# Seven products over two steps, two alternating banks, sums without GpSimd, weights kept as differences

## Chip, cores and metric

The kernel runs on one core of a Trainium2 chip. The metric is device time in microseconds: 755.94 us in the median of three runs (754.37 to 757.52). One further execution was recorded by the hardware profiler; it took 754.39 us.

## Reference

Two parts follow each other. The first is an attention with 32 memory slots per head (batch 8, 8 heads, 576 rows, head width 64):

```
a = softmax(phi)                 # over the 576 rows, per slot
k_m = a^T k ; v_m = a^T v        # 32 slots per head
attn = softmax(q k_m^T / 8)      # over the 32 slots
x = attn v_m                     # laid out as (4608, 512)
```

The second is a gated network on all 4608 rows, with weights of 512 x 1536 (two) and 1536 x 512:

```
out = (sigmoid(x w_gate) * (x w_val)) w_out
```

All arrays are fp32. The kernel never builds x: it multiplies v_m into the weights of gate and value first (that product is called U) and then multiplies U by the turned attention matrix `at`.

## The kernel before, in words

Every fp32 operand of the large matmuls is split into two fp32r parts, hi and lo (`x = hi + lo`), and every product is three matmuls: hi with hi, hi with lo, lo with hi. A hi part is a cast on ScalarE (ACT), a lo part a subtraction on VectorE (DVE).

The hidden width of 1536 is worked in 12 blocks f of 128, the rows in batch elements b of 576. The first stage does b = 0 to 3, in turns of four blocks for one element; the order of its instructions on DVE and ACT is planned at build time, except where the code chains them. Partial output sums go to DRAM and come back through four buffers called `row` (`row_of`, `leave`), stored from GpSimd's (POOL) queue and loaded on the queue of SyncE (SP). On the steps that begin with the third turn of b = 0 the weights of two blocks each are copied to DRAM (`kept_w`, six stores of 1 MB, L1188), also on SP, which works in order.

The second stage does b = 4 to 7, twelve steps each, one (b, f) after the other; the loop begins at L1301. `step` chains each engine's instructions in the order in which the code lists them, so PE, DVE, ACT and POOL each work in order there. For these elements gate and value of a block are computed together, as a 2 x 2 block product with seven products in place of eight (Winograd's form): the 576 rows in two halves of 288, gate and value as the two halves of the other side. `raw_at` holds the four blocks of the turned attention matrix and four sums of them (`sums_at`); `pair_u` makes U of two neighbouring blocks with 16 small matmuls into two PSUM banks, `u_out` copies them out (r and l), `u_sums` forms their sums (s), `part_hi` and `part_lo` split r, l and s. A pair is made one step ahead of its use.

The class `Group` is one step. `first` computes four products into banks c, d, a, b:

```
self.product(self.c, "s1", "t1", True)     # P5
self.product(self.d, "s3", "t3", True)     # P7
self.product(self.a, "a11", "b11", True)   # P1
self.product(self.bb, "s2", "t2", True)    # P6
```

`copies` moves P5, P7 and P1 to SBUF on ACT; `base` adds P6 and P1 on DVE; `corner` adds P5, P7 and that base on POOL (two adds); `second` adds P3, P4 and P2 onto banks c, d and a; `add` adds the base to c and d on DVE. `gate` takes the two sigmoids on ACT, `product_of` multiplies value by gate on DVE, `to_hi`, `to_left` and `to_lo` split the result. `out_half` multiplies a finished block by the output weights: two output tiles of 128 rows, three matmuls of 512 columns each, into four banks `acc`. In even steps two tiles stand between `first` and `second`, in odd steps none (L1330). `late_sides` spreads the softmax, the turning and the memory of the next two elements over the steps of the present one; `LEFT_AT` places the output of the 64 left-over rows of each element (`out_left`, 12 matmuls of 512 columns at a time).

POOL does the two adds of `corner`, the four sums of `u_sums`, the lo part of r and `sums_at` (L1145, L1146, L1076 to L1079, L1086, L931 to L934).

Of the kernel before, what the change touches and what calls it, by code (L numbers as in the profile page):

```python
# [17 lines left out]
P = 128  # L18
# [3 lines left out]
NKT = 4  # L22
# [76 lines left out]
def attn_moe_kernel(  # L99
# [27 lines left out]
    def bank():  # L127
        if "banks" in pools:
            return late_bank("b")
# [319 lines left out]
    def scores(b, c):  # L449

        n = cut(b, c).stop - cut(b, c).start
        pb = [late_bank("a"), late_bank("b")] if "banks" in pools else [bank(), bank()]
# [272 lines left out]
    def leave(b, f, t):  # L725
# [3 lines left out]
        if (b, t) in part:  # L729
            nc.vector.tensor_tensor(st, o, st, op=ALU.add)  # L730
            part.pop((b, t))
        elif t % 2:
            nc.scalar.copy(st, o)
        else:
            nc.vector.tensor_copy(st, o)  # L735
# [28 lines left out]
    def out_left(pair, f0, nf):  # L764
# [14 lines left out]
        for x in range(0, DM, n):  # L779
            xs = slice(x, x + n)  # L780
            st, o = left_sum[pair][:, xs], (late_bank("a") if x else bank())[:, :n]
# [256 lines left out]
    def pair_u(n, pb):  # L1038
# [7 lines left out]
        u = pairs_of[n] = {"pb": pb}  # L1046
# [16 lines left out]
    def u_out(n):  # L1063

        u = pairs_of[n]
        u["r"], u["l"] = late_tile("r_raw", 512), late_tile("l_raw", 512)
        nc.scalar.copy(u["r"], u["pb"][1])
        nc.vector.tensor_copy(u["l"], u["pb"][0])

    def u_sums(n, eng):  # L1070

        u = pairs_of[n]
        u["s"] = late_tile("s_raw", 768)
        l, r = [u[x].rearrange("p (f w x) -> p f w x", f=2, w=2) for x in "lr"]
        s = u["s"].rearrange("p (j f x) -> p j f x", j=3, f=2)
        eng.tensor_tensor(l[:, :, 1], l[:, :, 1], r[:, :, 1], op=ALU.add)  # L1076
        eng.tensor_tensor(s[:, 0], l[:, :, 1], l[:, :, 0], op=ALU.subtract)
        for w in range(2):
            eng.tensor_tensor(s[:, 1 + w], r[:, :, w], s[:, 0], op=ALU.subtract)  # L1079
# [4 lines left out]
    def part_lo(n, name, eng=None):  # L1084
        hi, lo = of_pair(n, name)
        (eng or nc.vector).tensor_tensor(lo, pairs_of[n][name], hi.bitcast(F32), op=ALU.subtract)  # L1086

    def operand(n, name, fi):
# [3 lines left out]
            "a11": ("l", fi * 256), "s1": ("l", fi * 256 + P),  # L1092
            "s2": ("s", fi * P), "s4": ("s", 256 + fi * P), "s3": ("s", 512 + fi * P),
# [11 lines left out]
    class Group:  # L1105
# [13 lines left out]
        def first(self):  # L1119
            self.c, self.d, self.a, self.bb = [late_bank(x)[:, :HALF] for x in "cdab"]  # L1120
            self.product(self.c, "s1", "t1", True)
            self.product(self.d, "s3", "t3", True)
            self.product(self.a, "a11", "b11", True)
            self.product(self.bb, "s2", "t2", True)

        def copies(self):
# [3 lines left out]
            self.p7 = late_tile("c_p7", HALF)  # L1130
            self.z = lp[0].tile([P, 4, HALF], F32, name="z", bufs=2)
            nc.scalar.copy(self.p5, self.c)  # L1132
            nc.scalar.copy(self.p7, self.d)  # L1133
            nc.scalar.copy(self.s1, self.a)  # L1134

        def base(self):
            nc.vector.tensor_tensor(self.x, self.bb, self.s1, op=ALU.add)  # L1137

        def second(self):
            self.product(self.c, "s4", "b22", False)  # L1140
            self.product(self.d, "a22", "t4", False)
            self.product(self.a, "a12", "b21", False)

        def corner(self):
            nc.gpsimd.tensor_tensor(self.p5, self.p5, self.p7, op=ALU.add)  # L1145
            nc.gpsimd.tensor_tensor(self.z[:, 3], self.p5, self.x, op=ALU.add)  # L1146

        def add(self, i):
            nc.vector.tensor_tensor(self.z[:, 1 + i], (self.c, self.d)[i], self.x, op=ALU.add)  # L1149

        def gate(self, i):
            curve(self.z[:, i], self.z[:, 1] if i else self.a, AF.Sigmoid)

        def product_of(self):
            nc.vector.tensor_tensor(self.z[:, 2:4], self.z[:, 2:4], self.z[:, 0:2], op=ALU.mult)  # L1155
# [20 lines left out]
    for i, (b, f, at_start, at_end) in enumerate(steps[:MAIN]):  # L1176
# [10 lines left out]
        if 0 <= k < NP:  # L1187
            move(kept_w[k], wg[:, 2 * k : 2 * k + 2].rearrange("p f k n -> p (f k n)"))  # L1188
# [23 lines left out]
        while len(pend) >= LAG:  # L1212
# [3 lines left out]
        if i >= MAIN - 2:  # L1216
            k = i - (MAIN - 2)
            pair_u(k, [bank(), bank()])
            u_out(k)
            u_sums(k, nc.vector)  # L1220
            for name in "lrs":
                part_hi(k, name)
                part_lo(k, name)
            if k == 0:
                out_half(*pend.pop(0))
# [10 lines left out]
    def out_next():  # L1236
        if pend:
            step(out_half, *pend.pop(0))

    def turn_at(b, i):  # L1240
        at_hi(b, i)
        at_lo(b, i)

    def late_sides(b):
# [6 lines left out]

        if n < B:
            soft = [s_max(n, c) for c in range(2)]
            norm = normalize(n)
            for c in range(2):
                put(2 * c + 2, "p", scores, n, c)
                put(2 * c + 2, "p", to_blocks, n, c)
                put(2 * c + 3, "z", next, soft[c])
                put(2 * c + 3, "z", next, soft[c])
            put(6, "a", s_exp, n)  # L1260
            put(7, "z", next, norm)
            put(8, "z", next, norm)
            put(9, "z", cross, n)
            put(10, "a", sums_at, n, nc.gpsimd)
        def go(k=1):
            for _ in range(k):
                next(memories[m])

        def end_n(k=1):
            for _ in range(k):  # L1270
                next(memories[n])

        if QUAD + 1 < n < B:
            put(0, "m", end_n)
            put(0, "mc", end_n, 2)
        if m < B:
# [3 lines left out]
            put(3, "z", a_max, m)  # L1280
            put(6, "a", a_exp, m)
            put(6, "z", a_sum, m)
            put(6, "z", begin_m)
            for f, place in ((7, "m"), (8, "m"), (9, "m"), (10, "m")):
                put(f, place, go)
                put(f, "mc", go)
            if m + 1 < B:
                put(10, "z", load_next, m + 1)
# [3 lines left out]
        (4, 6): (1, 0), (4, 11): (1, 4), (5, 6): (1, 8), (5, 11): (2, 0), (6, 6): (2, 4), (6, 11): (2, 8),  # L1292
        (7, 6): (3, 0), (7, 10): (3, 4),
    }

    for i in (1, 0):
        step(turn_at, QUAD, i)
    raw_at.pop(QUAD)
    load_q(QUAD + 1)
    out_next()  # L1300
    for b, f in [(b, f) for b in range(QUAD, B) for f in range(NFT)]:  # L1301
# [8 lines left out]
        odd = f % 2  # L1310
        turning = f == NFT - 1 and b + 1 < B
        g = Group(b, f)
        step(g.first)
        step(g.copies)
        step(g.base)
        step(g.corner)
        ready = 0 < n + 1 < NPAIRS and n > 0
        busy = f in (6, 7) and b + 1 < B
        if ready and not odd and not busy:
            for name in "rl":  # L1320
                step(part_hi, n + 1, name)
            step(part_lo, n + 1, "r", nc.gpsimd)
            step(part_lo, n + 1, "l")
            step(part_hi, n + 1, "s")
        if ready and odd and busy:
            for name in "lrs":
                step(part_hi, n + 1, name)
            step(part_lo, n + 1, "l")
        side("a")
        if not odd:  # L1330
            out_next()
        step(g.second)
        if (b, f) in LEFT_AT:
            step(next, run_left)
        side("m")
        step(g.add, 0)
        step(g.add, 1)
        step(g.gate, 0)
        if turning:
            step(at_hi, b + 1, 1)  # L1340
        side("mc")
        step(g.gate, 1)
        if turning:
            step(at_lo, b + 1, 1)
            step(at_hi, b + 1, 0)
        if (b, f) in LEFT_AT:
            step(next, run_left)
        if ready and not odd and not busy:
            step(part_lo, n + 1, "s")
        step(g.product_of)  # L1350
        if turning:
            step(at_lo, b + 1, 0)
        out_next()
        side("p")
        if ready and odd and busy:
            step(part_lo, n + 1, "s")
            step(part_lo, n + 1, "r", nc.gpsimd)
        step(g.to_hi)
        if odd and n + 2 < NPAIRS:
            step(pair_u, n + 2, [late_bank("a"), late_bank("b")])  # L1360
            step(u_out, n + 2)
            step(u_sums, n + 2, nc.gpsimd)
        step(g.to_left)
        if turning:
            raw_at.pop(b + 1)
            if b + 2 < B:
                load_q(b + 2)
        step(g.to_lo)
        if odd:
            out_next()  # L1370
        side("z")
        if (b, f + 1) in LEFT_AT:
            run_left = out_left(*LEFT_AT[b, f + 1], TURN)
            step(next, run_left)
        pend.extend((b, f, c, f == 0, f == NFT - 1) for c in range(2))
        if odd:
            pairs_of.pop(n)
# [58 lines left out]
```

## Time and profile before

| | us |
|---|---|
| median of three runs | 755.94 |
| lowest, highest | 754.37, 757.52 |
| the profiled execution | 754.39 |
| its span, first to last instruction | 752.5 |
| PE busy (matmuls) | 715.0, 95% of the span |
| DVE busy | 544.2, 72% |
| ACT busy | 409.4, 54% |
| POOL busy | 246.6, 33% |

Busy time is time in which an engine had an instruction under way. A matmul's end is modelled, and matmuls overlap, so 95% of PE is not 95% of its peak. The second stage begins at 379 us and ends at about 740 us; POOL works in it for 212 us and hardly before it. The granted clock of PE is full but for a few us, 0.98 on average in the stretch from 564.9 to 657.5 us. Every stall is shown by the engine that waits and by what released it.

### The profile page before, as it was taken

Reading aid. Unit: us, or ns where it says so; the run is one execution under the profiler, and the core shown is the slowest. Engines: PE = TensorE matmul, PEld = TensorE weight load, DVE = VectorE, ACT = ScalarE, POOL = GpSimd, SP = SyncE. Lnnn points to the kernel's source line nnn. Section 1 sums busy time; section 2 is a strip of 40 time slices with the busy share of each in tenths; the row PEclk is TensorE's granted clock in tenths of the full one; section 3 lists DMA queues with packets and bytes.
Section 4 is the critical chain, followed back from the end, with each engine's and each line's share of the span. In section 5 each row is a group of like instructions: output and inputs, shape, how many; then the busy total and the mean of one; then the engine's idle time right before and its main releaser. Section 6 shows DMA issues by size and latency. Waiting matters only on the chain.

```text
span 752.5 us, 14249 instructions
## 1 busy us (share of the span) xinstructions
PE 715.0 (95%) x5524; PEld 582.7 (77%) x5524; DVE 544.2 (72%) x907; ACT 409.4 (54%) x937; POOL 246.6 (33%) x289
## 2 busy tenths in 40 slices
PE   8899999999999999999999989999899998898997
PEld 7557788888888898888877767778677787677786
DVE  4999998667787545486478787697776868776554
ACT  4676865455444433354555765647656465464552
POOL 0000100120211011001046466664667556675450
PEclk9999999999999999999999999999999999999999
DMA  8985549567545689232483115612116112141102
GB/s 351 421 352 194 198 143 380 162 225 278 182 161 207 224 311 329 92 105 99 140 329 116 57 57 214 231 58 70 57 57 231 57 57 92 51 153 57 57 1 70
DMA packets 31858, 124.64 MB, mean 166 GB/s; under 512 B 3952, under 2 KB 5232, under 8 KB 25264
## 3 DMA queue, kind: packets, MB, share of 16 engines
q1 hardware_dynamic: 25696, 103.03, 37.6%
q0 software_dynamic: 6096, 20.71, 7.7%
q8 instruction: 43, 0.70, 0.4%
q14 instruction: 23, 0.19, 0.1%
HBM read 94.90 MB, written 28.84 MB: 164 GB/s over the span
## 4 chain that ended last, share of the span: by engine, by line
PE 65%; DVE 16%; ACT 7%; issue 6%; POOL 2%; DMA 2%; SPq 0%; DVEq 0%; ACTq 0%; POOLq 0%
PE acc L189 26%; PE pu_t L189 24%; PE a L189 5%; PE b L189 5%; DVE z L1155 4%; PE c L189 3%; PE d L189 2%; DMA kvm<-in_kvm_dram 2%; DVE z L1149 1%; ACT s_hi L1082 1%; ACT c_p L1132 1%; DVE e L499 1%; DVE e L482 1%; DVE e L473 1%; ACT u_hi L1082 1%
## 5 line engine op out<-in xcount | busy, mean ns | idle before, releaser
L189 PE MATMUL pu_t<-at,u_hi 128*128 128x320 f32 (+1 forms) x752 | 156.1, 303 | 0.2 <-DVE sg L670 0.2
L189 PE MATMUL acc<-wo_hi,g_hi 128*128 128x512 f32 x372 | 151.3, 407 | 0.0
L189 PE MATMUL acc<-wo_hi,g_lo 128*128 128x512 f32 x372 | 146.7, 394 | 0.0
L189 PE MATMUL acc<-wo_lo,g_hi 128*128 128x512 f32 x372 | 146.6, 394 | 0.0
L189 PEld LDWEIGHTS pu_t<-at,u_hi 128*128 128x128 f32 x752 | 124.3, 188 | 11.0 <-issue 2.1
L189 PE MATMUL pu_t<-at,u_lo 128*128 128x320 f32 (+1 forms) x360 | 106.2, 295 | 0.0
L189 PEld LDWEIGHTS acc<-wo_hi,g_hi 128*128 128x128 f32 x372 | 69.9, 188 | 37.6 <-issue 28.5
L164 ACT ACTIVATE sg<-pu_t 128x256 f32<-128x256 f32 (+1 forms) x94 | 38.7, 412 | 81.7 <-PE pu_t L189 81.5
L189 PEld LDWEIGHTS acc<-wo_hi,g_lo 128*128 128x128 f32 x372 | 69.9, 188 | 16.6 <-DVE g_lo L179 0.2
L670 DVE TENSOR_TENSOR sg<-pu_t,sg 128x256 f32<-128x256 f32 (+1 forms) x92 | 41.5, 454 | 52.5 <-ACT sg L164 35.5
L189 PEld LDWEIGHTS acc<-wo_lo,g_hi 128*128 128x128 f32 x372 | 70.1, 188 | 9.1
L1145 POOL TENSOR_TENSOR c_p<-c_p,c_p 128x288 f32<-128x288 f32 x48 | 46.3, 964 | 90.3 <-ACT c_p L1133 90.3
L1160 ACT CAST g_hi<-z 128x512 fp32r<-128x512 f32 x48 | 29.7, 619 | 77.6 <-DVE z L1155 77.6
L175 POOL DMA_DIRECT2D part<-row x32 | 17.7, 555 | 157.9 <-DVE row L735 82.7
L189 PEld LDWEIGHTS pu_t<-at,u_lo 128*128 128x128 f32 x360 | 67.8, 188 | 0.0
L680 ACT CAST g_hi<-sg 128x256 fp32r<-128x256 f32 x90 | 36.5, 407 | 47.9 <-DVE sg L670 46.7
L1155 DVE TENSOR_TENSOR z<-z 128x576 f32<-128x576 f32 x48 | 45.5, 948 | 15.3 <-ACT z L164 12.0
L1146 POOL TENSOR_TENSOR z<-c_p,c_x 128x288 f32<-128x288 f32 x48 | 45.8, 955 | 4.9 <-DVE c_x L1137 1.2
L179 DVE TENSOR_TENSOR g_lo<-sg,g_hi 128x256 fp32r<-128x256 f32 x90 | 37.4, 418 | 12.1 <-ACT g_hi L680 12.1
L1076 POOL TENSOR_TENSOR l_raw<-l_raw,r_raw 128x256 f32<-128x256 f32 x22 | 22.9, 1039 | 66.8 <-ACT left L1170 58.1
L179 DVE TENSOR_TENSOR g_lo<-z,g_hi 128x512 fp32r<-128x512 f32 x48 | 34.1, 710 | 11.2 <-ACT g_hi L1160 11.0
L1137 DVE TENSOR_TENSOR c_x<-b,c_s 128x288 f32<-128x288 f32 x48 | 21.6, 450 | 25.8 <-ACT c_s L1134 25.7
(255 smaller groups left out, 1615.8 us busy)
## 6 DMA issues: line engine op xcount, KB each, us to landing
ring<-wgv SPq DMA_DIRECT2D x24, 1024.0 KB, 4.8
at<-at SPq DMA_DIRECT2D x24, 576.0 KB, 6.3
kvm<-in_kvm_dram SPq DMA_DIRECT2D x12, 1024.0 KB, 10.6
q<-in_qT_dram SPq DMA_DIRECT2D x16, 512.0 KB, 8.2
part<-row POOLq DMA_DIRECT2D x32, 256.0 KB, 4.9
row<-part SPq DMA_DIRECT2D x32, 256.0 KB, 3.9
wgv<-wg SPq DMA_DIRECT2D x6, 1024.0 KB, 10.9
wg<-in_kvm_dram SPq DMA_DIRECT2D x4, 1024.0 KB, 11.7
```

The source lines that it names most:

```text
L164: last_act[0] = nc.scalar.activation(*args, **kw)
L175: last_move[queue] = queues[queue].dma_start(dst, src)
L179: return nc.vector.tensor_tensor(lo, x, hi.bitcast(F32), op=ALU.subtract)
L189: last_pe[0] = do(*args, **kw)
L670: last_prod[0] = nc.vector.tensor_tensor(prod, ps[1][:, :n], sg[:, :n], op=ALU.mult)
L680: nc.scalar.copy(hi, prod[:, : 2 * P])
L1076: eng.tensor_tensor(l[:, :, 1], l[:, :, 1], r[:, :, 1], op=ALU.add)
L1137: nc.vector.tensor_tensor(self.x, self.bb, self.s1, op=ALU.add)
L1145: nc.gpsimd.tensor_tensor(self.p5, self.p5, self.p7, op=ALU.add)
L1146: nc.gpsimd.tensor_tensor(self.z[:, 3], self.p5, self.x, op=ALU.add)
L1155: nc.vector.tensor_tensor(self.z[:, 2:4], self.z[:, 2:4], self.z[:, 0:2], op=ALU.mult)
L1160: nc.scalar.copy(self.g[0], self.z[:, 2:4, : 2 * P])
```

## The change

The seven products of a step get other banks and another order. P1 opens bank d (in odd blocks bank b); ACT copies it (`c_s1`); P6 is added onto the same bank, ACT copies the sum (`c_x`); one step later P7 is added, DVE adds P5 to it (the corner), then P4 is added and DVE multiplies straight out of the bank. P5 opens bank c and P3 is added to it; P2 has bank a alone. So P7 and P4 of a block are computed in the step of the next block, except at an element's last block (f = 11), where they follow at once. `corner`, `base` and POOL's part of `u_sums` and `part_lo` are gone; `copies` is one copy at a time. Both sigmoids read SBUF; the product of value and gate is two operations of 288 columns in place of one of 576.

`pair_u` moves into even steps, one pair ahead, on banks c and a; `u_out` copies both on ACT; `u_sums` is three sums on DVE, since the stored weights already hold a difference: in the `kept_w` copy partitions 0 to 63 hold gate minus value in the columns of value, made by two DVE subtractions into `row` buffers. Each of the six stores becomes four: partitions 64 to 127 whole, the left columns of partitions 0 to 63, and one for each of the two differences.

Output is issued by single tiles (`out_tile`), three or four per step, with sides and left-over work at new places. All finished tiles leave by ACT in the second stage. The second element's pair of the first stage's end (pair 1) is made inside the loop, and queries are loaded at the end of f = 0.

```diff
+        elif t % 2 or "banks" in pools:
             nc.scalar.copy(st, o)
-    def u_sums(n, eng):
...
+    def u_out(n, name):
+        u = pairs_of[n]
+        u[name] = late_tile(f"{name}_raw", 512)
+        nc.scalar.copy(u[name], u["pb"]["lr".index(name)])
+    def u_sums(n, *which):
...
+        for j in which:
+            x, y, op = [
+                (r[:, :, 1], l[:, :, 1], ALU.subtract),
+                (s[:, 0], l[:, :, 0], ALU.add),
+                (r[:, :, 0], s[:, 0], ALU.subtract),
+            ][j]
+            nc.vector.tensor_tensor(s[:, j], x, y, op=op)
...
+        def p(self, n):
+            where, x, t, start = {
+                1: ("d", "a11", "b11", True), 2: ("a", "a12", "b21", True), 5: ("c", "s1", "t1", True),
+                6: ("d", "s2", "t2", False), 3: ("c", "s4", "b22", False), 7: ("d", "s3", "t3", False),
+                4: ("d", "a22", "t4", False),
+            }[n]
+            if start:
+                name = "b" if where == "d" and self.f % 2 else where
+                setattr(self, where, late_bank(name)[:, :HALF])
+            self.product(getattr(self, where), x, t, start)
+        def copy(self, name):
+            nc.scalar.copy(getattr(self, name), self.c if name == "p5" else self.d)
         def add(self, i):
-            nc.vector.tensor_tensor(self.z[:, 1 + i], (self.c, self.d)[i], self.x, op=ALU.add)
+            x, y = {0: (self.a, self.s1), 1: (self.c, self.x), 3: (self.d, self.p5)}[i]
+            nc.vector.tensor_tensor(self.z[:, i], x, y, op=ALU.add)
...
+        def product_of(self, i):
+            x = (self.d, self.z[:, 3])[i]
+            nc.vector.tensor_tensor(self.z[:, 2 + i], x, self.z[:, i], op=ALU.mult)
...
-            move(kept_w[k], wg[:, 2 * k : 2 * k + 2].rearrange("p f k n -> p (f k n)"))
+            w, kept_k = wg[:, 2 * k : 2 * k + 2], kept_w[k].rearrange("p (f k n) -> p f k n", f=2, k=NKT)
+            move(kept_k[D:], w[D:])
+            move(kept_k[:D, :, :, :P], w[:D, :, :, :P])
+            for j in range(2):
+                t = mb.tile([P, DM], F32, name="row", bufs=4)[:D]
+                t = t.rearrange("p (k n) -> p k n", k=NKT)
+                nc.vector.tensor_tensor(t, w[:D, j, :, :P], w[:D, j, :, P:], op=ALU.subtract)
+                move(kept_k[:D, j, :, P:], t)
```

The new step, in its order (h is the group of the block before, `more` means that another pair follows):

```diff
+        if h:
+            step(h.p, 7)
+        step(g.p, 1)
+        if h:
+            step(h.add, 3)
+        step(g.copy, "s1")
...
+        if not odd and more:
+            step(pair_u, n + 1, [late_bank("c"), late_bank("a")])
+            step(u_out, n + 1, "r")
+            step(u_out, n + 1, "l")
+        side("m")
+        side("m3")
+        step(out_tile)
+        if wide:
+            step(out_tile)
+        if h:
+            step(h.product_of, 1)
+        side("act")
...
+        step(g.p, 2)
+        step(g.p, 5)
+        if odd and more:
+            step(part_lo, n + 1, "r")
+        step(g.add, 0)
+        step(g.copy, "p5")
+        if odd and more:
+            step(part_lo, n + 1, "l")
...
+        side("B")
+        if not wide:
+            step(out_tile)
+        if h:
+            step(h.p, 4)
+        step(g.p, 6)
+        if h:
+            step(h.product_of, 0)
+        step(g.copy, "x")
+        if h:
+            step(h.to_hi)
+            step(h.to_left)
+        if not odd and more:
+            step(u_sums, n + 1, 0, 1)
+        step(out_tile)
...
+        step(g.p, 3)
...
+        step(g.add, 1)
...
+        if turning:
+            step(g.p, 7)
+            step(g.add, 3)
+        if h:
+            step(h.to_lo)
+        if turning and b + 1 < B:
+            step(at_lo, b + 1, 0)
+        step(g.gate, 0)
+        step(g.gate, 1)
...
+        if f > 1:
+            step(out_tile)
+        side("Z")
...
+        if turning:
+            step(out_tile)
+            step(g.product_of, 1)
+            step(g.p, 4)
+            if b + 1 < B:
+                step(at_hi, b + 1, 1)
+                step(at_lo, b + 1, 1)
+                raw_at.pop(b + 1)
+            step(g.product_of, 0)
+            step(g.to_hi)
...
```

In `late_sides` the softmax pieces of the next element stand at "B" and "Z" (f = 3 to 9), the scores at "m" of f = 3 and 5, the exponentials at "act" of f = 7, the memory at f = 8 to 11, the crossing at "B" of f = 10.

## Rows read from the trace of the kernel before

**Rows 1.** Stretches b = 4 to 7: length, busy (instructions) by engine, clock, DMA.
```profile
379.20:472.00 92.80, 86.94 (x671) 69.67 (x670) 73.65 (x109) 55.30 (x125) 53.95 (x58) 1.00 0.42 157
472.00:564.90 92.90, 87.12 (x675) 70.17 (x674) 71.16 (x102) 57.53 (x129) 56.74 (x59) 1.00 0.27 96
564.90:657.50 92.60, 85.00 (x586) 68.25 (x585) 70.31 (x99) 53.34 (x119) 57.80 (x59) 0.98 0.27 96
657.50:740.00 82.50, 76.29 (x476) 63.63 (x475) 51.65 (x78) 42.95 (x105) 44.06 (x49) 1.00 0.18 64
```
**Rows 2.** Waits of PE from 365 us on: total us, times, longest.
```profile
PE c L189 <- ACT c_p L1132: 18.9, 14, 2.6
PE a L189 <- DVE e L473: 5.1, 6, 1.1
```
**Rows 3.** Timeline, PE, one pair of steps in b = 7: start, length, instruction.
```profile
657.46 0.42 PE L189 MATMUL c<-at,s_hi 128*128 128x288 f32 x2
...
659.05 0.40 PE L189 MATMUL acc<-wo_hi,g_hi 128*128 128x512 f32 x1
...
660.44 0.42 PE L189 MATMUL c<-at,s_hi 128*128 128x288 f32 x2
...
666.29 0.53 PE L189 MATMUL c<-at,s_hi 128*128 128x288 f32 x2 [1.51 <-ACT c_p L1132]
...
668.76 0.40 PE L189 MATMUL acc<-wo_hi,g_lo 128*128 128x512 f32 x1
...
670.11 0.50 PE L189 MATMUL acc<-wo_hi,g_hi 128*128 128x512 f32 x1
...
671.61 0.42 PE L189 MATMUL c<-at,u_hi 128*128 128x288 f32 x2
```
**Rows 4.** Timeline, POOL, DVE and ACT, in the same pair.
```profile
662.52 2.01 POOL L1086 TENSOR_TENSOR u_lo<-r_raw,u_hi 128x512 fp32r<-128x512 f32 x1
...
663.30 1.85 DVE L1155 TENSOR_TENSOR z<-z 128x576 f32<-128x576 f32 x1
...
665.18 0.62 ACT L1160 CAST g_hi<-z 128x512 fp32r<-128x512 f32 x1 [1.37 <-DVE z L1155]
...
665.85 0.39 ACT L1132 COPY c_p<-c 128x288 f32<-128x288 f32 x1
666.14 0.40 ACT L1133 COPY c_p<-d 128x288 f32<-128x288 f32 x1
```
**Rows 5.** Groups by shape, 379 to 742 us: count, busy us, mean ns, idle before.
```profile
L1155 DVE TENSOR_TENSOR z<-z 128x576 f32<-128x576 f32 x48 | 45.5, 948 | 15.3 <-ACT z L164 12.0 <-POOL z L1146 3.1
...
L1149 DVE TENSOR_TENSOR z<-c,c_x 128x288 f32<-128x288 f32 x48 | 21.7, 452 | 3.8 <-PE c L189 1.3
...
L482 DVE TENSOR_TENSOR e<-e,mx 128x576 f32<-128x576 f32 x6 | 8.0, 1328 | 0.2
L164 ACT ACT_TABLE_LOAD x6 | 7.7, 1283 | 0.1
L1082 ACT CAST s_hi<-l_raw 128x512 fp32r<-128x512 f32 x11 | 6.9, 628 | 0.0
L939 ACT CAST at<-q 128x1152 fp32r<-128x1152 f32 x6 | 6.9, 1146 | 0.0
```
**Rows 6.** The same view, 150 to 379 us.
```profile
L179 DVE TENSOR_TENSOR u_lo<-pu_t,u_hi 128x512 fp32r<-128x512 f32 x32 | 19.9, 682 | 10.5 <-ACT u_hi L593 10.5
...
L1079 DVE TENSOR_TENSOR s_raw<-r_raw,s_raw 128x256 f32<-128x256 f32 x2 | 0.8, 418 | 0.0
```
**Rows 7.** Timeline of SP's DMA issues, first stage.
```profile
257.42 2.29 SPq L175 DMA_DIRECT2D wgv<-wg  x4
274.36 1.90 SPq L175 DMA_DIRECT2D row<-part  x4
```
**Rows 8.** Timeline of POOL's DMA issues, first stage.
```profile
266.46 1.23 POOL L175 DMA_DIRECT2D part<-row  x2 [20.77 <-DVE row L730]
...
292.65 1.14 POOL L175 DMA_DIRECT2D out_dram<-row  x2 [22.13 <-DVE row L730]
```

More of the change, by code (lines that the diff above doesn't have):

```diff
@@ L1117, in product, with tiles @@
                 )
[L1119 to L1126, printed above, removed]
+        def tiles(self):
             self.s1, self.p5, self.x = [
@@ L1234, in attn_moe_kernel, with put_tiles, out_tile @@
     pools["banks"] = banks.enter_context(tc.tile_pool(name="late_banks", bufs=1, space=PSUM, reuse_waits="tile"))
[L1236 to L1242, printed above, removed]
+    tiles = []
+    def put_tiles(b, f, c, at_start, at_end):
+        tiles.extend((b, f, 2 * c + j, at_start, at_end) for j in range(2))
+    def out_tile():
+        if not tiles:
+            return
+        b, f, t, at_start, at_end = tiles.pop(0)
+        hi, lo = [x[:, (t % 2) * P : (t % 2 + 1) * P] for x in G[b, f, t // 2]]
+        w_hi, w_lo = wo_of(f)
+        if at_start:
+            acc[b, t] = po.tile([P, DM], F32, name=f"acc{t}")
+        for i, (l, r) in enumerate([(hi, w_hi), (hi, w_lo), (lo, w_hi)]):
+            matmul(acc[b, t], l, r, start=at_start and i == 0, stop=at_end and i == 2)
+        if at_end:
+            leave(b, f, t)
     def late_sides(b):
@@ L1250, in put, with go @@
             plan.setdefault((f, place), []).append((do, args))
+        def go(x, k=1):
+            for _ in range(k):
+                next(memories[x])
         if n < B:
+            if n > QUAD + 1:
+                put(0, "m2", go, n)
+                put(0, "end", go, n, 2)
             soft = [s_max(n, c) for c in range(2)]
@@ L1309, in attn_moe_kernel @@
         n = (b - QUAD) * NP + f // 2
-        odd = f % 2
-        turning = f == NFT - 1 and b + 1 < B
+        odd, turning = f % 2, f == NFT - 1
+        more = n + 1 < NPAIRS
         g = Group(b, f)
[L1313 to L1322, printed above, removed]
-            step(part_lo, n + 1, "l")
-            step(part_hi, n + 1, "s")
@@ L1325, in attn_moe_kernel @@
[L1325 to L1336, printed above, removed]
-        step(g.add, 1)
-        step(g.gate, 0)
-        if turning:
[L1340 to L1377, printed above, removed]
-    run_left = out_left(B // 2 - 1, 2 * TURN, TURN)
@@ new lines, in attn_moe_kernel @@
+        side("B")
[13 more added lines that the diff above has]
+        step(out_tile)
+        side("m2")
+        if late_left:
+            step(next, extra, None)
+        step(g.p, 3)
+        side("end")
+        if turning and b + 1 < B:
+            step(at_hi, b + 1, 0)
@@ new lines, in attn_moe_kernel @@
+        if not odd and more:
+            step(part_hi, n + 1, "r")
+        if odd and more:
+            step(part_hi, n + 1, "s")
+        step(g.add, 1)
+        if late_left:
+            step(next, extra, None)
+        if turning:
[3 more added lines that the diff above has]
+            step(h.to_lo)
+        if turning and b + 1 < B:
+            step(at_lo, b + 1, 0)
+        step(g.gate, 0)
+        step(g.gate, 1)
+        if not odd and more:
+            step(u_sums, n + 1, 2)
+            step(part_hi, n + 1, "l")
@@ L1385 @@
+    extra = out_left(B // 2 - 1, 2 * TURN, TURN)
+    step(next, extra)
+    while tiles:
+        step(out_tile)
+    step(next, extra)
 _INS = ["qT", "kvm", "kvt", "phiT", "wgv", "wo"]
```

156 lines of the change are left out of this document (75 added, 81 removed).

## The prediction, made before the result was known

> **What bounds the kernel now.** I read the busy time by stretch first, one stretch for each batch element b = 4 to 7 of the second stage [rows 1]: TensorE (PE) is busy 85 to 87 us of each 92.6 to 92.9 us, VectorE (DVE) 70 to 74, ScalarE (ACT) 53 to 58, GpSimd (POOL) 54 to 58. No other engine comes near PE, yet PE has holes. Its waits name them [rows 2]: 18.9 us in 14 waits for the ACT copy out of bank c (L1132), 5.1 us in 6 waits for the transposes of the scores (L473).
>
> Busy time flatters PE, because a matmul's end is modelled. So I counted what its work needs, from starts of one pair of steps [rows 3]. Four products lie between 657.46 and 659.05, 0.40 us each; two output tiles between 659.05 and 660.44, 0.70 each (three matmuls of 0.23). The small U matmuls of a pair with their change-overs: from the tile matmul at 668.76 to the next at 670.11 is 1.35, less that matmul's own 0.23, is 1.12. One batch element has 84 products (33.4), 48 tiles (33.4), 6 U (6.7), 24 matmuls of left-over rows (24 x 0.23 = 5.6), and for b = 4 and 5 some 4.5 of scores and memory work, for b = 6 some 1.5 (estimates from their matmul counts): 83.6, 83.6 and 80.6 us. For b = 7, without the last two U and with 45 tiles inside the stretch, 74.6. Against 92.8, 92.9, 92.6 and 82.5 [rows 1] that leaves 9.2, 9.3, 12.0 and 7.9: 38 us of the stage in which PE does nothing useful. The two waits of [rows 2], 24.0 us, are the visible part; every wait hides some 0.2 more behind a modelled end, and change-overs of 0.1 make up part of the rest. In b = 6 the granted clock averages 0.98 [rows 1], some us at 1.2 instead of 2.4 GHz, at most 1.9 us of its 12.0; I count it as part of the holes. I call 36 removable.
>
> The chain behind a c wait stands in [rows 4]. POOL makes the low part of r for 2.01 us from 662.52; the DVE product L1155 starts at 663.30 and takes 1.85, where its mean is 0.95 [rows 5]; the ACT cast of g waits 1.37 for it; the copy of bank c stands behind that cast on ACT's queue and starts at 665.85; PE, done with the fourth product at about 664.6, starts the next at 666.29 [rows 3]. So what PE needs next is queued behind what only the output needs later.
>
> **The change part by part.**
>
> *Products over two steps.* The seven products, 48 tiles and 6 U per element are the same matmuls: nothing on PE is added or removed. What changes is the distance between a product and the copy that frees its bank. I walked a plain even step with the slots above; P7 and P4 belong to the group before: P7 0 to 0.4, P1 0.8, U 1.9, two tiles 3.3, P2 3.7, P5 4.1, P4 4.5, P6 4.9, tile 5.6, P3 6.0, tile 6.7. A result is readable 0.2 after its slot. P6 needs P1 copied: 1.0 + 0.4 = 1.4, starts 4.5. P2 needs the copy of r: 2.2 + 0.6 = 2.8, starts 3.3; P5 that of l: 3.4, starts 3.7. P3 needs P5 copied: 4.7, starts 5.6. The next P7 needs P1+P6 copied: 5.5, starts 6.7. P4 needs the DVE add of the corner: 1.1, starts 4.1. The bank of the next P1 is free after the product with P4: 5.2, needed 7.1. The low part of g is done about 7.4; the tile that multiplies it does so at 8.0. An odd step (no U, one tile fewer there) is 5.6 us long and has the same distances without U. So no wait falls on PE in a plain pair; the tightest are the 0.3 and 0.5 us at the copies of l and r.
>
> *Work moved from POOL.* POOL loses two adds per step, four sums and half of the low parts per pair. DVE takes three sums of 256 columns at 0.42 and the low part of r (0.69) [rows 6], and gives the copy of l (0.69) to ACT, which pays some 0.6. DVE by whole durations: per step five operations of 288 columns at 0.45 [rows 5] and g's low part 0.69; per pair also three sums and the low parts of r, l, s (0.69, 0.69, some 1.0 by width): 9.5 us of a pair's 12.3. ACT: 7 to 9 us of 12.3. Both are hidden by PE; uncovered, DVE's moved work would be about 2 us per pair. No price is left on the path here.
>
> *Side work (softmax, memory, turning).* The plain walk has no room for it, so I placed it. On f = 5 and 7, DVE comes from a step with the subtraction of 1.33 [rows 5] before the product that frees P1's bank, and f = 5 also needs bank c for the scores: some 1.0 and 0.5 us of PE wait. On f = 7 ACT changes tables twice (1.28 each) [rows 5] and runs the exponentials, with P5's copy and then r's copy behind them: 0.1 to 1.8. At f = 0 the copy of r stands behind the last group's cast, which stands behind the second half's ACT cast of the turned matrix (1.15 [rows 5]), its low part and a product on DVE: 1.6 to 2.5. Taking ACT and DVE operations as far apart as they start (0.29 for a copy of 0.39, at 665.85 and 666.14 [rows 4]) the sum is 3.3 per element, by whole durations 6.6. I take 4 for b = 4 to 6, near the measured spacing, and 1 for b = 7, which has no side work.
>
> *The ends.* Pair 1's U is made inside the stage instead of before it, the same work elsewhere: nothing. Queries are loaded at the end of f = 0 and used at f = 3, some 16 us later: nothing. All copies of finished tiles go to ACT: four of 0.6 per element, inside its idle time.
>
> *Weights stored as differences.* Six stores of 1 MB become six times a store of partitions 64 to 127, one of the other partitions' left columns, and two DVE subtractions with a store each. They lie in the first stage, where SP issued four of the old stores in 2.29 us from 257.42 and the next load of partial sums at 274.36 [rows 7]. The twelve new tiles come from the four "row" buffers that the partial sums use, whose stores POOL issues at 266.46 and after [rows 8]. DVE pays 12 x 0.7 = 8 us, under PE's time. The unseen price is order: SP now waits for each subtraction, a subtraction waits for a row to be stored, and DVE, in order, stands meanwhile; behind it are the products that free PE's banks. Below: 0, since PE shows no wait in this stretch. Above: two rounds of the 7.9 us between a row's store at 266.46 and its next load at 274.36, 16. I take 1.5, nearer to 0, because the rows loaded at 274.36 leave again only at 292.65 [rows 8], 18 us later.
>
> The Trainium skill (SBUF — State Buffer, "Door 1: The DMA port swizzle") says a transfer on partitions 0 to 63 reaches only half of the ports, measured there as 196 GB/s against 328 for all 128. By that rule, an estimate from the page, the six megabytes take some 13 us of transfer time more. No run here shows half-partition stores yet. By the rule all on the path the sum would end 13 us later; by the rows, which show no PE wait there, it stays.
>
> *Sum.* 36 removable, minus 3 x 4 + 1 = 13 that stay or appear, is 23; minus 1.5 in the first stage is 21.5. The profiled execution took 754.39 us (span 752.5, 1.9 around it): 732.9. The median of the three runs is 1.5 above that execution, so I say 734.
>
> **The rivals.**
>
> *Side work eats it.* DVE is already busy for 70 to 74 of 93 us in b = 4 to 6; if their waits only change their names, the gain is b = 7's 7.9 - 1, less 1.5: 750. For it: the waits there include softmax and turning. Against: DVE's time holds waiting for POOL, as the 1.85 shows.
>
> *Row buffers.* The first stage pays the upper 16 instead of 1.5: 748. For it: in-order SP and DVE share four buffers. Against: 18 us of slack.
>
> *All of it.* PE never waits: 754.4 - 36 = 718, about 720 with the run's offset. Against: the f = 0 chain.
>
> *ACT's queue (slower).* In every even step P2 and P5 wait for two copies in a row on ACT that used to be shared with DVE. Cover is 0.5 us. An ACT late by x costs 24 x (x - 0.5). It decides at x = 2.0, where 36 us are given back; at x = 2.5 the time is 754 - 36 + 48 = 766, and 768 against the median. For it: ACT now carries the copies of l and all tiles, with casts of 0.63 [rows 5] ahead of the copies in its queue. Against: by the walk ACT ends an odd step's casts about 0.8 before the next U is readable.
>
> **How the numbers follow.** Two kernels differ measurably from about half a per cent, 3.8 us. Forecast (724 to 744) 0.54; all of it 0.07; side work 0.13; row buffers 0.07: 0.81 together, of which 0.01 ends within the bound, so faster 0.80. Several small losses that meet the gain: 0.07, so no change 0.08. ACT's queue: 0.12. From 721 to 754 leaves out 2 in 10: most of the slower rival, part of no change, the tip of the full gain.
>
> **What would show it.** Right: the waits for c_p (L1132) gone from PE's list; a plain pair near 12.3 us where it was 14.15 (657.46 to 671.61 [rows 3]); POOL near zero arithmetic; DVE operations from SBUF no longer stretched; b = 7 about 75 us long. Waits left at f = 0, 5, 7, of 0.5 to 2 us. Wrong: PE waiting for the copies of r and l in plain even steps; DVE waiting in the first stage for a row, with PE behind it; a pair above 13.5 us in b = 7.

## The result and the profile after

The changed kernel takes 733.32 us (median of 4 runs, 733.25 to 733.34), the kernel before 755.33 beside it (754.37 to 757.52): a ratio of 0.970, 95% interval 0.968 to 0.973. The profiled execution took 733.32 us, its span 731.5, against 754.39 and 752.5 before.

The page after, busy time of each engine. PE went up to 97% of the span, POOL fell to 83 instructions:

```profile
span 731.5 us, 14167 instructions
PE 713.2 (97%) x5524; PEld 582.4 (80%) x5524; DVE 536.3 (73%) x1021; ACT 421.0 (58%) x969; POOL 47.5 (6%) x83
```

The second stage by element, b = 4 to 7, the columns as in [rows 1]:

```profile
376.80:464.30 87.50, 86.77 (x670) 70.21 (x669) 68.40 (x132) 56.97 (x131) 5.93 (x8) 1.00 0.42 155
464.30:553.30 89.00, 87.42 (x674) 70.52 (x673) 67.99 (x131) 60.13 (x138) 3.76 (x4) 1.00 0.29 100
553.30:639.80 86.50, 84.00 (x585) 67.46 (x584) 66.36 (x127) 55.80 (x127) 3.75 (x4) 1.00 0.30 103
639.80:719.70 79.90, 78.58 (x499) 65.31 (x498) 54.14 (x110) 48.32 (x117) 0.00 (x0) 1.00 0.19 67
```

DVE's busy time fell although DVE took over work from POOL: 68.4 where it was 73.7 in b = 4. Against [rows 1] the elements are 5.3, 3.9, 6.1 and 2.6 us shorter; b = 7 is the odd one because it now holds 23 matmuls more (499 against 476): the 16 small ones of one more U and some tiles. Of the 21.0 us of span, 2.4 come before the first product of b = 4 (which starts at 376.78 after 379.20), 17.4 in the stage up to the last product (342.9 after 360.3), 1.2 behind it. Matmuls moved between these parts: the stage took one U (1.1 us) and three tiles (2.1) from its neighbours, so for equal work it is 20.6 us shorter, and the first part, which gave up one U and two tiles, some 2.5 us of work, is shorter by just that.

PE's waits from 370 us on, to be set against [rows 2]:

```profile
PE a L189 <- ACT r_raw L1067: 3.5, 3, 1.3
PE acc L189 <- DVE g_lo L179: 1.4, 2, 1.1
PE a L189 <- ACT row L388: 0.9, 2, 0.4
PE c L189 <- DVE z L1143: 0.3, 1, 0.3
```

The 18.9 us for c_p are gone, and so are the 5.1 for the scores' transposes. In their place stand 6.1 us, more than half of it three waits for the copy of r at f = 0.

A plain pair of steps in b = 7 (timeline, PE: start, length), from the product P2 of f = 2 to that of f = 4, where [rows 3] had 14.15 us:

```profile
655.24 0.42 PE L189 MATMUL a<-at,u_hi 128*128 128x288 f32 x2
...
667.55 0.42 PE L189 MATMUL a<-at,s_hi 128*128 128x288 f32 x2
```

It takes 12.31 us, and no instruction between waits for another engine.

### The profile page after: what moved, and what is told of

Read it like the earlier page. It is cut to its first block, busy times and chain, and to the rows that moved or that the text cites. A ratio compares the mean times of both kernels' runs of the same rounds, so it can differ in the third digit from the quotient of the medians.

```text
span 731.5 us, 14167 instructions
## 1 busy us (share of the span) xinstructions
PE 713.2 (97%) x5524; PEld 582.4 (80%) x5524; DVE 536.3 (73%) x1021; ACT 421.0 (58%) x969; POOL 47.5 (6%) x83
## 4 chain that ended last, share of the span: by engine, by line
PE 82%; DVE 11%; ACT 3%; DMA 2%; issue 1%; SPq 0%; DVEq 0%; ACTq 0%
PE acc L189 33%; PE pu_t L189 25%; PE c L189 8%; PE a L189 7%; PE d L189 4%; PE b L189 4%; DMA kvm<-in_kvm_dram 2%; DVE zs L495 1%; DVE at L179 1%; DVE z L1143 1%; DVE z L1150 1%; DVE e L482 1%; DVE e L499 1%; DVE mx L480 1%; DVE e L473 1%
## 5 line engine op out<-in xcount | busy, mean ns | idle before, releaser
L1139 ACT COPY c_p<-c 128x288 f32<-128x288 f32 x48 | 19.2, 400 | 56.7 <-PE c L189 56.7
L1155 ACT CAST g_hi<-z 128x512 fp32r<-128x512 f32 x48 | 29.8, 621 | 29.7 <-DVE z L1150 29.7
L1143 DVE TENSOR_TENSOR z<-c,c_x 128x288 f32<-128x288 f32 x48 | 21.8, 454 | 31.3 <-PE c L189 24.6
L1143 DVE TENSOR_TENSOR z<-a,c_s 128x288 f32<-128x288 f32 x48 | 21.9, 456 | 30.2 <-PE a L189 28.9
L164 ACT ACTIVATE z<-z 128x288 f32<-128x288 f32 x96 | 38.2, 438 | 8.5 <-DVE z L1143 8.2
L179 DVE TENSOR_TENSOR u_lo<-pu_t,u_hi 128x512 fp32r<-128x512 f32 (+1 forms) x46 | 28.6, 672 | 10.4 <-ACT u_hi L593 10.4
L593 ACT CAST u_hi<-pu_t 128x512 fp32r<-128x512 f32 (+1 forms) x46 | 24.0, 587 | 13.8 <-PE pu_t L189 13.7
```

What stands on the lines that cost most here:

```text
L164: last_act[0] = nc.scalar.activation(*args, **kw)
L179: return nc.vector.tensor_tensor(lo, x, hi.bitcast(F32), op=ALU.subtract)
L593: nc.scalar.copy(hi[:, r, :nf], U[b, fs[0], "pb"][r])
L1139: nc.scalar.copy(getattr(self, name), self.c if name == "p5" else self.d)
L1143: nc.vector.tensor_tensor(self.z[:, i], x, y, op=ALU.add)
L1155: nc.scalar.copy(self.g[0], self.z[:, 2:4, : 2 * P])
```

## The experiments

Theory A, the prediction's: the holes were the distance in the queues between a product and the copy that frees its bank, and the chain over two steps in two banks removes them. Theory B: they were GpSimd's contention with VectorE, and what helps is that GpSimd does no arithmetic. Theory C: the new order of the side work would do alone.

**GpSimd busy beside it, for nobody** (POOL's arithmetic of the kernel before, as many and as wide, on a tile that nobody reads):

```
+            step(nc.gpsimd.tensor_tensor, spin[:, :n_cols], x, spin[:, :n_cols], op=ALU.subtract)
```

> The changed kernel, with arithmetic on GpSimd added that nobody waits for: in every step two subtractions of 288 columns (the first reads the step's copy of the first product), in odd steps four of 256 and in even ones one of 512, as many and as wide as the kernel before had. Theory A (the holes were the distance in the queues: chain over two steps): GpSimd's presence beside VectorE costs little, 733 to 737 us, PE waits in the second stage at most some 3 us above the changed kernel's. Theory B (what went was GpSimd's contention with VectorE): 742 to 748 us, VectorE's subtractions of low parts visibly longer and PE's holes back by 8 us or more.

735.9 us (735.8 to 737.0), 2.6 more. The contention is real; by-shape groups of DVE in the second stage, this run:

```profile
L1150 DVE TENSOR_TENSOR z<-z 128x288 f32<-128x288 f32 x48 | 26.2, 546 | 5.7 <-ACT z L164 2.4
...
L179 DVE TENSOR_TENSOR s_lo<-r_raw,s_hi 128x512 fp32r<-128x512 f32 x11 | 12.2, 1106 | 0.0
```

The same groups in the changed kernel:

```profile
L1150 DVE TENSOR_TENSOR z<-z 128x288 f32<-128x288 f32 x48 | 21.7, 453 | 5.6 <-ACT z L164 2.4
...
L179 DVE TENSOR_TENSOR s_lo<-r_raw,s_hi 128x512 fp32r<-128x512 f32 x11 | 7.5, 683 | 0.0
```

546 ns for 453, 1106 for 683: DVE's instructions take longer, but DVE has room, and PE gives back little of its 20 us. Theory A.

**The old order without GpSimd** (the kernel before; POOL's additions, sums and low part of r on DVE in place):

```
-        nc.gpsimd.tensor_tensor(self.p5, self.p5, self.p7, op=ALU.add)
+        nc.vector.tensor_tensor(self.p5, self.p5, self.p7, op=ALU.add)
...
-                step(u_sums, n + 2, nc.gpsimd)
+                step(u_sums, n + 2, nc.vector)
```

> The kernel before, its chain of sums in one step as it was, with GpSimd's arithmetic of the steps (the corner's two additions, the pair's sums, the low part of r) on VectorE at the same places of the order. Theory B: most of the gain, 735 to 742 us. Theory A: the holes stay, since the chain from the last product to the next step is as long and VectorE's queue is longer by some 5 us a step: 750 to 762 us.

755.0 us (754.7 to 757.9), ratio 0.999 (0.998 to 1.001): nothing. L1155, at 948 ns in [rows 5], takes 754 here, and still PE waits (from 365 us on):

```profile
PE c L189 <- ACT c_p L1132: 11.4, 14, 1.6
PE c L189 <- DVE z L1149: 5.8, 7, 2.0
PE a L189 <- DVE e L473: 3.4, 3, 1.2
PE acc L189 <- DVE g_lo L179: 2.7, 4, 0.9
```

The wait for c_p is shorter, and what it lost, others have: DVE's own queue is now in the chain. Theory B falls as it was put, that having no arithmetic on GpSimd is what helps. The old order with that work on neither engine was not run, so what contention alone cost there stays open.

**The sums on GpSimd again** (the changed kernel, only the pair's sums and the low part of r moved back):

```
-            nc.vector.tensor_tensor(s[:, j], x, y, op=op)
+            eng.tensor_tensor(s[:, j], x, y, op=op)
```

> The changed kernel with the pair's three sums and the low part of r on GpSimd again, in the places that they have now. Theory A: there is a whole step between them and their readers, so 733 to 738 us. Theory B: GpSimd beside VectorE is the cost, and 740 us or more. A third reading (GpSimd's own latency, 2.0 us for the low part of r, reaches the products of the next pair): a wait of PE at the first product that reads the sums, and 738 to 745 us.

731.3 us (731.1 to 731.8), ratio 0.968 (0.966 to 0.970): not slower than the change but 2.0 us faster, which none of the three readings had. The wait for the g_lo that is made at f = 10 of b = 6 is gone; DVE's queue lost 30 us of work in the stage. So this part of the change was a small loss.

**The chain drained inside its step** (the turning step's ending in every step; the rest of the change kept):

```
-        if turning:
-            step(g.p, 7)
-            step(g.add, 3)
+        step(g.p, 7)
+        step(g.add, 3)
...
+        step(g.product_of, 1)
+        step(g.p, 4)
+        step(g.product_of, 0)
+        step(g.to_hi)
+        step(g.to_left)
+        step(g.to_lo)
```

> The changed kernel with the chain of sums drained inside its own step, in every step as in the turning one (seventh product, corner, gates, product of sums, fourth product, cast, low part), and all else kept: no GpSimd arithmetic, the alternating banks, the side work's places, the weights as differences. Theory A (the spread over two steps removes the waits): from the end of the third product to the fourth there are an addition of 0.46, two gates of 0.44 and a multiplication of 0.45 with three hand-overs, some 1.9 us, against 1.1 us of products and a tile that TensorE has: 0.8 us or more in 44 steps, 765 to 775 us. Theory C (the side work's new places and the shorter chain would do without the spread): 733 to 742 us.

761.8 us (761.6 to 761.9), ratio 1.007 (1.005 to 1.009): 28.5 above the change, and slower than the kernel before. PE's waits:

```profile
PE d L189 <- DVE z L1143: 16.0, 19, 1.3
PE b L189 <- DVE z L1143: 5.6, 10, 1.6
PE a L189 <- ACT r_raw L1067: 4.2, 9, 1.1
```

The time is 3 us below my band, and my chain was wrong: the fourth product waits for the corner's addition (L1143), which reads the bank behind the seventh product, 29 visible waits of some 0.75 us; it needs neither gates nor multiplications. Theory C falls; the spread is worth 28 us with all else in place. That is more than the whole gain, so this is what the spread is worth within the new order, not a return to the old one.

**One bank** (the same, and the chain's sums always in bank d):

```
-                name = "b" if where == "d" and self.f % 2 else where
-                setattr(self, where, late_bank(name)[:, :HALF])
+                setattr(self, where, late_bank(where)[:, :HALF])
```

> The kernel of the chain in one step, with that chain's sums in the same bank in all steps instead of two in turn. If the second bank matters: the next step's first product waits until the last multiplication has read the bank, 0.45 us and the hand-overs behind the fourth product, some 0.7 us in 44 steps: 30 us above the run with two banks. If the first product is late anyway: the same time within 5 us.

834.6 us (830.4 to 834.9), 73 above two banks where 30 were expected. PE's waits, and its four stretches (length, busy by engine, clock):

```profile
PE d L189 <- DVE z L1149: 47.6, 47, 2.6
PE d L189 <- DVE z L1142: 20.7, 28, 1.3
```

```profile
376.70:493.30 116.60, 97.11 (x671) 73.95 (x669) 71.15 (x135) 59.87 (x132) 5.79 (x8) 0.94 0.31 117
493.30:608.80 115.50, 96.06 (x674) 73.46 (x674) 68.04 (x130) 62.66 (x138) 3.62 (x4) 0.96 0.22 77
608.80:725.20 116.40, 97.03 (x585) 72.71 (x585) 66.64 (x127) 58.68 (x128) 3.63 (x4) 0.91 0.22 76
725.20:821.30 96.10, 86.07 (x498) 66.39 (x499) 51.19 (x105) 49.41 (x115) 0.00 (x0) 0.97 0.16 55
```

47 waits of 1.0 us for the last multiplication: the first product of every step. Visible waits are 42.5 us more than in the run before; most of the rest is the clock, which was 1.00 in all four stretches there. 116.6 x 0.06 + 115.5 x 0.04 + 116.4 x 0.09 + 96.1 x 0.03 = 25 us of its cycles were missing here; some 5 us of the 73 stay open. The second bank was tried with the chain in one step alone, not with the chain over two.

**The weights stored whole** (one store each as before; l0 - l1 by one more DVE subtraction per pair):

```
+        if 0 in which:
+            nc.vector.tensor_tensor(l[:, :, 1], l[:, :, 0], l[:, :, 1], op=ALU.subtract)
```

> The changed kernel with the weights of pairs 0 to 16 stored whole in one transfer as before, no differences; the difference l0 - l1 is taken in the second stage instead, by one more VectorE subtraction in each pair's sums (24 of some 0.4 us). The prediction's term: storing differences costs 1.5 us, so 731 to 733 us. Rival (row buffers and SP's queue cost much): 725 us or less. If the stores cost nothing, 733 to 735 us.

738.5 us (737.0 to 738.6): 5.2 slower, against all expectations. The first product starts at 376.85, against 376.78: storing differences costs nothing. The price lies in the second stage; its worst place is the g_lo made at f = 10 of b = 6, for which PE waits in f = 11 (PE, 630 to 640 us; then clock and busy time just behind it):

```profile
PE acc L189 <- DVE g_lo L179: 2.1, 1, 2.1
```

```profile
636.80:640.20 3.40, 3.40 (x11) 3.01 (x12) 2.65 (x6) 0.77 (x3) 0.00 (x0) 0.50 0.00 0
```

PE stood for 2.1 us, and the 3.4 us behind that ran at 1.2 GHz (granted clock 0.50): 1.7 us more, in this execution.

**One more subtraction, unread** (the differences kept; a DVE instruction at that place whose result nobody uses):

```
+        if 0 in which and n:
+            nc.vector.tensor_tensor(spare_sum, l[:, :, 0], l[:, :, 1], op=ALU.subtract)
```

> The changed kernel, its weights as differences, with one more VectorE subtraction ahead of each pair's sums (l0 - l1 once more, 256 columns, 0.42 us alone), which nobody reads. It tells apart why storing the weights whole came out 5 us slower. If that instruction's place in VectorE's queue is the price (in the step of f=10 it runs beside GpSimd, at some 1.0 us, ahead of the low part that a tile waits for): 736 to 739 us, the wait for g_lo at f=10 of the element before the last 1.5 to 2.1 us. If the price is the chain through it (the sums read its result) or the stored data: 733 to 734 us.

735.8 us (735.2 to 737.1): 2.5 above the change, by its place in the queue alone, a little under the band I gave for that. DVE beside POOL's four additions, this run:

```profile
630.98 1.04 DVE L1077 TENSOR_TENSOR spare_sum<-l_raw 128x256 f32<-128x256 f32 x1
631.95 1.03 DVE L1084 TENSOR_TENSOR s_raw<-r_raw,l_raw 128x256 f32<-128x256 f32 x1
633.01 0.90 DVE L1084 TENSOR_TENSOR s_raw<-s_raw,l_raw 128x256 f32<-128x256 f32 x1
...
634.21 0.91 DVE L179 TENSOR_TENSOR g_lo<-z,g_hi 128x512 fp32r<-128x512 f32 x1
635.04 0.41 DVE L1084 TENSOR_TENSOR s_raw<-r_raw,s_raw 128x256 f32<-128x256 f32 x1
```

A sum of 256 columns takes 1.0 us while POOL works and 0.41 when it has stopped. PE's wait for that g_lo is 2.1 us here as well, but the clock stayed at 1.00 behind it. Single executions at the full clock can be set side by side: 733.3 for the change, 735.2 here, 737.0 with whole weights. By them 1.9 us of the 5.2 are the place in the queue and 1.8 the rest of that edit, most likely the chain through the subtraction, whose result the sums read; that was not measured by itself. The last 1.5 are the clock: the other three executions with whole weights took 738.4 to 738.6 at a mean of 0.997 or 0.998.

**l copied by VectorE** (the rival "ACT's queue"):

```
-        nc.scalar.copy(u[name], u["pb"]["lr".index(name)])
+        (nc.scalar.copy if name == "r" else nc.vector.tensor_copy)(u[name], u["pb"]["lr".index(name)])
```

> The changed kernel with l copied out of its bank by VectorE, as in the kernel before, in place of ScalarE. Rival of the prediction (ScalarE's queue has become the bound of the even steps): 731 us or less. Theory A (ScalarE has room, VectorE's queue is the tighter one, and the copy of 0.68 us stands ahead of the product of sums there): 734 to 738 us.

733.4 us (733.3 to 733.4): no change, below my 734 to 738 too. The copy has slack on either engine; ACT's queue is no bound.

**The low part behind the product** (turning step; the chain at f = 0 put to the test):

```
                 step(at_hi, b + 1, 1)
-                step(at_lo, b + 1, 1)
-                raw_at.pop(b + 1)
             step(g.product_of, 0)
+            if b + 1 < B:
+                step(at_lo, b + 1, 1)
+                raw_at.pop(b + 1)
```

> The changed kernel with one DVE instruction moved in the turning step: the low part of the second half of the next element's at (1.35 us) goes behind the last product of sums instead of ahead of it. If the chain read off the trace is right (product of sums, cast g_hi, copy of c_s, copy of r_raw, then TensorE's second product), the three waits of 1.3 us at f=0 go to at most 0.2: 729.5 to 731 us. If the copies of the pair's U are late for another reason, the waits stay: 733 us. If the fifth product then waits for the low part that now comes later, it takes their place: 732 to 734 us.

730.0 us (729.5 to 730.8), ratio 0.965 (0.964 to 0.967). The chain in the changed kernel, start of b = 6:

```profile
554.24 1.35 DVE L179 TENSOR_TENSOR at<-q,at 128x1152 fp32r<-128x1152 f32 x1
...
555.51 0.46 DVE L1150 TENSOR_TENSOR z<-b,z 128x288 f32<-128x288 f32 x1
...
556.00 0.62 ACT L1155 CAST g_hi<-z 128x512 fp32r<-128x512 f32 x1 [2.12 <-DVE z L1150]
...
556.96 0.59 ACT L1067 COPY r_raw<-a 128x512 f32<-128x512 f32 x1
...
557.60 0.53 PE L189 MATMUL a<-at,s_hi 128*128 128x288 f32 x2 [1.12 <-ACT r_raw L1067]
```

and with the two DVE instructions exchanged:

```profile
554.08 0.46 DVE L1150 TENSOR_TENSOR z<-b,z 128x288 f32<-128x288 f32 x1
...
554.45 1.35 DVE L179 TENSOR_TENSOR at<-q,at 128x1152 fp32r<-128x1152 f32 x1
...
554.57 0.62 ACT L1155 CAST g_hi<-z 128x512 fp32r<-128x512 f32 x1 [0.85 <-DVE z L1150]
...
555.53 0.59 ACT L1067 COPY r_raw<-a 128x512 f32<-128x512 f32 x1
```

The copy of r comes 1.4 us earlier, and its wait is gone from PE's list: the chain was read rightly.

**Both** (the last, and the sums on GpSimd), the two diffs in one:

```
-                step(at_lo, b + 1, 1)
             step(g.product_of, 0)
+                step(at_lo, b + 1, 1)
...
-            nc.vector.tensor_tensor(s[:, j], x, y, op=op)
+            eng.tensor_tensor(s[:, j], x, y, op=op)
```

> The changed kernel with both: the pair's three sums and the low part of r on GpSimd (731.3 us alone), and the low part of at behind the product of sums in the turning step. If the two gains are of different places (VectorE's queue, and the wait at f=0 behind the cast), they add: 727.5 to 729.5 us. If both shorten the same wait: 731 us.

727.8 us (727.76 to 727.85), ratio 0.962 (0.961 to 0.964), the fastest here. The gains add (2.0 and 3.3 of 5.5).

**Then the block's additions on VectorE too**:

```
-            put(10, "Z", sums_at, n, nc.gpsimd)
+            put(10, "Z", sums_at, n, nc.vector)
```

> The fastest so far (the pair's sums and the low part of r on GpSimd, the low part of at behind the product of sums; 727.8 us) with the four additions over the block's exponentials at f=10 on VectorE instead of GpSimd. If VectorE beside GpSimd is what is left there (g_lo 1.29 us in place of 0.68, a wait of 0.9 us at the first product of f=11): 726.5 to 727.5 us. If four more instructions of 0.42 us in VectorE's queue cost as much: 727.5 to 729 us.

728.6 us (728.4 to 728.9): 0.8 slower, inside the second band. PE's list has one wait more, 0.7 us for a DVE addition (L1144) that reads bank d. Whatever DVE gains by POOL's absence there, four more instructions in its own queue cost more.

**The fastest, with whole weights and the fourth sum on GpSimd**:

```
+        if 0 in which:
+            eng.tensor_tensor(l[:, :, 1], l[:, :, 0], l[:, :, 1], op=ALU.subtract)
```

> The fastest so far (727.8 us) with the weights stored whole, as before, and the fourth sum l0 - l1 taken on GpSimd ahead of the pair's other three (0.73 us each there). If the differences save only VectorE's place in the queue, GpSimd has room for the fourth sum and the time is the same: 727.5 to 729 us. If the chain through the fourth sum is the price (it must be done before the cast of l, and the odd step's products read that), the casts stand later in ScalarE's queue: 731 us or more.

731.9 us (731.8 to 732.2): 4.1 slower, by neither of the two reasons given. POOL's fourth sum reaches into a DVE instruction that has nothing to do with it (POOL and DVE, end of f = 4 of b = 4):

```profile
407.36 1.18 POOL L1084 TENSOR_TENSOR s_raw<-r_raw,s_raw 128x256 f32<-128x256 f32 x1
```

```profile
407.88 1.29 DVE L482 TENSOR_TENSOR e<-e,mx 128x576 f32<-128x576 f32 x1
409.08 0.45 DVE L1153 TENSOR_TENSOR z<-b,z 128x288 f32<-128x288 f32 x1
```

In the fastest run, where POOL's sums end at 406.97, the same subtraction takes 0.75. Here it begins inside POOL's sum and ends 0.63 us behind that sum's end (408.54); so the last multiplication is late, and the next step's own first product (P1) waits for its bank, 3.9 us in 6 waits. All six have this subtraction, at 1.29, just ahead of them.

## Why the prediction was right, by its steps

The mechanism held: the waits for c_p are gone, and taking the spread out alone brings waits back. That the sum came so near is in part luck, since two of its terms were each some 5 us off and cancel.

**The holes (36 removable).** The mechanism was right, the size was not. Counted over the whole stage from starts, against the unit costs of the prediction, PE's gaps were 41.8 us before and 19.7 after. Those longer than 0.15 us fell from 30.7 (30 of them) to 8.1 (12); the rest, mostly steps of some 0.1 us at change-overs, was 11.1 and is 11.6. So 30.7 could go, not 36: I had counted change-overs as holes. Seven of the 30, 1.5 us together, are matmuls at a granted clock of 0.50 from 649.0 to 652.4 us, behind the longest wait for c_p (2.6 us); after the change the stage has no such stretch.

**The side work (13 stay).** Mis-sized the other way: 8.1 stay. At f = 0 the three waits are 1.27, 1.28 and 1.47 us from start to start, by the chain foretold, under its 1.6 to 2.5. At f = 5 and at f = 7 no gap is left. The price of 1.0 and 0.5 there came from the subtraction's 1.33 us [rows 5], and that was a duration under POOL's load; the 0.1 to 1.8 for ACT's tables and exponentials at f = 7 came to nothing as well. (The upper ends that the prediction lists add up to 5.8, not to its 6.6; no term shows the rest.) The subtraction's group after the change:

```profile
L482 DVE TENSOR_TENSOR e<-e,mx 128x576 f32<-128x576 f32 x6 | 4.5, 751 | 0.0
```

Taking it from before counted the disease that the change cures. Places I had not named pay instead: 0.6 at f = 9 twice (the copy of the memory transposes, L388), 1.3 for the g_lo made at f = 10 of b = 6, where DVE's sums stand behind POOL's four additions, 0.46 at f = 2 of b = 4 (U's bank c), and five of 0.2 to 0.4 for g_lo. The two errors, 5.3 too many removable and 4.9 too many staying, cancel: 22.6 net against 23. (The count does not close to the last us: by it the gaps are 22.1 less, by the stage's length at equal work 20.6.) The 1.5 us added for the median did not come: the profiled execution, 732.9 by the sum, took 733.32, and so did the median. The kernel before varies from 754.4 to 757.5; the changed one stays within 0.1 us.

**The plain pair.** 12.3 forecast, 12.31 to 12.36 measured in b = 7. The walk by slots held: no wait at the copies of l and r, whose slack it had put at 0.3 and 0.5.

**Work moved from POOL (no price on the path).** Nearly: it costs 2.0 us, since the tighter queue is DVE's and the sums have a whole step of time on POOL. (POOL gave up one of the three low parts of a pair, that of r, not half of them.)

**Weights as differences (1.5).** In the first stage 0, though SP's stores take the order feared; SP, first stage after the change, where [rows 7] had the load of partial sums at 274.36:

```profile
273.49 3.46 SPq L175 DMA_DIRECT2D wgv<-row  x2
...
286.75 2.32 SPq L175 DMA_DIRECT2D row<-part  x4
```

The load is 12.4 us later, inside the 18 us of slack. DVE does stand for a row, as feared: 0.6, 1.9 and 4.1 us before three of the subtractions, at 272, 278 and 300 us. But nothing on PE stands behind it: PE shows no wait from 240 to 377. By the port rule of the Trainium skill (SBUF — State Buffer, "Door 1: The DMA port swizzle") 13 us more of transfer were to come, by the prediction's estimate; whether they did isn't separated here, the path pays none. What I left out is what the differences save: a fourth sum in the step costs 4 to 5 us on either engine.

**The rivals.** "All of it" (720) stood against the f = 0 chain, as said: with that and the sums mended the time is 727.8, still not 720. "Side work eats it" (750) falls: b = 4 to 6 are 15.3 us shorter, not only b = 7. "Row buffers" and "ACT's queue" fall by the runs above.

**The signs.** One was missed: b = 7 was to be about 75 us long and is 79.9. Work moved into it makes 2.7 of that, its wait at f = 0 another 1.5; some 1 us is not accounted for one by one.

## What to carry to other kernels

When a bank's copy stands behind work that only the output needs, move the consumer a step on and give the chain a second bank: without the one, the change here loses 28 us, without the other as well, 73 more. Price what stays with durations from a stretch in which the load you remove is not running. An engine taken out altogether is not the aim: keep on GpSimd what has a step of slack, and place it where VectorE isn't on the path.

## What was not expected of the hardware

- A DVE operation on two SBUF tensors takes up to 2.5 times as long while GpSimd works: 0.41 and 1.04 us for 256 columns, 0.75 and 1.29 for the subtraction of 576. The traces show that it isn't slowed evenly but ends a fixed time behind POOL's instruction. POOL's four additions beside the DVE rows of "One more subtraction":

```profile
630.93 0.81 POOL L931 TENSOR_TENSOR q<-q 128x288 f32<-128x288 f32 x1 [84.60 <-DVE q L924]
631.82 0.87 POOL L932 TENSOR_TENSOR q<-q 128x288 f32<-128x288 f32 x1
632.77 0.86 POOL L933 TENSOR_TENSOR q<-q 128x288 f32<-128x288 f32 x1
633.59 0.97 POOL L934 TENSOR_TENSOR q<-q 128x288 f32<-128x288 f32 x1
```

The three DVE sums that begin inside the first three end 0.28, 0.29 and 0.28 us behind them, g_lo 0.56 behind the fourth: always some 0.13 less than they take alone (0.41 and 0.68). In the second stages of all 14 traces 393 DVE operations with both inputs in SBUF begin inside an arithmetic instruction of POOL; 392 of them end after it. So the price is what is left of POOL's instruction: a long one on POOL can cost DVE most. Additions that read a PSUM bank did not wait: L1143 at 631.61 us in the changed kernel, inside POOL's four, took 0.45, as elsewhere.
- PE's waits can cost twice, but not each time. After a wait of 2.1 us, 3.4 us ran at a granted clock of 0.50 (whole weights); after the same wait in "One more subtraction" the clock stayed at 1.00. In the kernel before, a wait of 2.4 us at 632.5 was not followed by a fall, one of 2.6 at 647.7 was. With 47 waits of 1.0 us and 28 of 0.7 the four stretches were granted 0.91 to 0.97, 25 us on top of the waits.
